# Gated attention and a feed-forward block on one core: pair 0 by token chunks, natural gates, one transfer queue and a new order

## The chip, the core and the metric

The kernel runs on one core of a Trainium2 chip. The metric is device time in microseconds of one execution, the median over runs. A profiled execution gives the span from the first to the last instruction and the busy time of each engine: PE (TensorE: matmuls and transposes; PEld is its weight load), DVE (VectorE), ACT (ScalarE), POOL (GpSimd), and SP (SyncE, which here only issues transfers). The transfers run on 16 DMA engines that all queues share.

## The reference

There are 4 batches, 8 heads, 768 tokens and 48 channels per head. A complex gate `a` with its magnitude capped at 0.999 decays a state per channel; `k` and `v` are added as an outer product, and `q` reads the state:

```python
mag = np.sqrt(a_re * a_re + a_im * a_im)
scale = np.minimum(mag, 0.999) / (mag + 1e-06)
for t in range(S):
    new_re = ar * S_re - ai * S_im
    new_im = ar * S_im + ai * S_re
    S_re, S_im = (new_re + einsum('bhd,bhe->bhde', k[t], v[t]), new_im)
    y[t] = einsum('bhd,bhde->bhe', q[t], S_re)
```

The heads' outputs are laid side by side (384 channels), and each token goes through a layer norm and a feed-forward block with a residual: `x + relu(norm(x) * g_ln @ w_ch1) @ w_ch2`, with 1536 hidden channels. Inputs and output are fp32.

## The kernel before

Tokens are handled in chunks of 128 (one token to a partition), and two chunks make a *pair*. A batch has three pairs, so there are 12 pairs, P = 0 to 11, and 24 chunks, n = 0 to 23. Pairs 0, 3, 6 and 9 begin a batch.

The recurrence is turned into matmuls. For a pair, the log magnitude `l` and the angle `th` of the gate are computed per token and channel; prefix sums over the tokens, which are matmuls with triangular ones, give the total decay and phase from the pair's start. Multiplying `k` and `q` by exponentials of these sums, and by cosine and sine, makes the recurrence an ordinary masked attention within the chunk plus a carried state `G`.

The steps of a pair have names that the plan uses, `name.P` or `name.n`, some with a part after them:

- `are`, `aim`, `q`, `k`, `vf`: loads. `ln`, `iv`, `r`: w = ln(re), 1/re, r = im/re. `r2`, `u`, `l`, `lc`: r squared, ln(1+r squared), half of it plus w, and the cap. `th`: arctan r.
- `dec`: matmuls that sum `l` over tokens; `e` and `en`: exponentials of plus and minus the sum. `ph`: the same sums of `th`, with the carry of the pair before; `sin`, `cos` (through `qt`, a quarter turn added on PE, or through `abs`); `car`: the carry to the next pair. `tab` loads ACT's function table (logarithms and exponentials, or trigonometry).
- `ke`, `qe`: k and q times the exponentials; `ks`, `qs`: times cosine and sine. `kT`, `qT` are transposes on PE and `ksT`, `qsT` their copies out of PSUM; where the plan gives `ksT` or `qsT` to SP, a transposing transfer does the whole step.
- `am`: scores, `atm`: scores times the mask, `gm`, `G`: the state, `y`: the output, `x`: its copy, `bn`: layer norm statistics, `rstd`: the inverse deviation, `xtr`, `xT`: x transposed.
- `mm1` (first product; three groups of four hidden blocks, two parts each), `relu`, `mm2` (second product, three parts for each chunk), `oa` and `ot`: scaling and residual, `st`: the store.
- `wl`, `wp`, `wc`: the weights are loaded as bf16 by POOL's queue, and g_ln and the mean's removal are folded into the first.

How the gates lie in SBUF matters for the change. `are` and `aim` are loaded so that a partition holds two *consecutive* tokens of the pair (a run of 384 B in DRAM). The sum for chunk c then takes both slots of every partition: `dec` is 2 x 2 matmuls with four triangular matrices `u_e[c, j]`, and `ph` likewise with `u_th`, plus one matmul for each chunk that adds the carry through `pick`. Pair 0 alone is cut in two parts by heads (`PARTS = {0: 2}`: four heads each), so that its first steps are shorter; both parts need both chunks of q and k.

The order is written by hand, as one list. A token `name:Ek` gives an operation to an engine (P = PE, A = ACT, V = DVE, G = POOL, S = SP) and, where it uses PSUM, to a bank; each engine runs its operations in the order of the list. A suffix `@other` makes an operation wait for another one ("turns at the shared port", for POOL and DVE). A transfer is issued by the engine that the token names, so that a wait in front of an issue holds up everything behind it in that queue. `warm.i` are fill-in matmuls that keep PE running and whose result isn't used. The buffers are rings (`RINGS`): three of `are`, `aim`, `q`, `k`, two of `vf`, five of `ot`.

Line 754 is `mm2`, 722 `mm1`, 617 `am`, 594 `kT` and `qT`, 688 `xtr`, 477 `dec`, 492 and 496 `ph`, 787 the fill-ins, 739 and 741 `relu`, 404 the loads of q, k and v, 445 those of the gates, 599 the transposing transfers, 777 the stores, 792 table loads, 770 `ot` on DVE; 295 and 292 are helpers for many of DVE's and POOL's products and copies.

Of the kernel before, what the change touches and what calls it, by code (L numbers as in the profile page):

```python
# [9 lines left out]
FP32 = mybir.dt.float32  # L10
# [24 lines left out]

ENGINES = {"P": "PE", "A": "ACT", "V": "DVE", "G": "POOL", "S": "SP"}
# [3 lines left out]
aim.0.0:A tab.log.0:A aim.0.1:A ue:G are.0.0:S are.0.1:S pad.e.1:G uth:V one:G warm.0:P0 pad.ks.0:G warm.1:P0  # L40
warm.2:P0 pick:G warm.3:P0 are.1.0:S warm.4:P0 warm.5:P0 warm.6:P0 k.0.1:S ln.0.0:A warm.7:P0 car0.1:G warm.8:P0
cmean:G iv.0.0:A warm.9:P0 ident:G warm.10:P0 warm.11:P0 r.0.0:V warm.12:P0 warm.13:P0 warm.14:P0 aim.1.0:S warm.15:P0
warm.16:P0 warm.17:P0 ln.0.1:A warm.18:P0 warm.19:P0 r2.0.0:A warm.20:P0 k.0.0:S warm.21:P0 warm.22:P0 warm.23:P0
warm.24:P0 u.0.0:A warm.25:P0 warm.26:P0 warm.27:P0 warm.28:P0 iv.0.1:A warm.29:P0 l.0.0:V warm.30:P0 are.2.0:S
warm.31:P0 warm.32:P0 ln.1.0:A warm.33:P0 warm.34:P0 r.0.1:G warm.35:P0 lc.0.0:V warm.36:P0 warm.37:P0 aim.2.0:S
warm.38:P0 warm.39:P0 warm.40:P0 iv.1.0:A warm.41:P0 warm.42:P0 pad.ks.1:G warm.43:P0 warm.44:P0 warm.45:P0 warm.46:P0
warm.47:P0 zdec:G r2.0.1:A warm.48:P0 pad.e.0:G warm.49:P0 pad.qs.0:G warm.50:P0 q.0.1:S warm.51:P0 warm.52:P0 u.0.1:A
warm.53:P0 warm.54:P0 r.1.0:V warm.55:P0 dec.0.0:P0 warm.56:P1 warm.57:P1 q.1.0:S e.0.0:A0 warm.58:P1 warm.59:P1
warm.60:P1 r2.1.0:V warm.61:P1 en.0.0:A0 warm.62:P1 warm.63:P1 warm.64:P1 l.0.1:V warm.65:P1 u.1.0:A warm.66:P1
warm.67:P1 warm.68:P1 warm.69:P1 lc.0.1:V warm.70:P1 are.3.0:S warm.71:P1 warm.72:P1 warm.73:P1 ln.2.0:A warm.74:P1  # L50
l.1.0:V warm.75:P1 warm.76:P1 warm.77:P1 warm.78:P1 dec.0.1:P6 q.1.1:S warm.79:P0 warm.80:P0 lc.1.0:V en.0.1:A6
warm.81:P0 warm.82:P0 warm.83:P0 warm.84:P0 q.0.0:S iv.2.0:A warm.85:P0 warm.86:P0 ke.0.1.0:G@lc.1.0 warm.87:P0
dec.1.0:P0 e.0.1:A6 r.2.0:V wl.1:G warm.88:P2 warm.89:P2 e.1.0:A0 warm.90:P2 warm.91:P2 warm.92:P2 warm.93:P2
warm.94:P2 gln:S r2.2.0:V en.1.0:A0 qrow:G dps.1:P4 dps.0:P5 ke.0.0.0:V warm.95:P2 warm.96:P2 u.2.0:A warm.97:P2
warm.98:P2 decc.1:V4 warm.99:P2 vf.0.0:S car0.0:G warm.100:P2 warm.101:P2 warm.102:P2 mask:G warm.103:P2 warm.104:P2
aim.3.0:S tab.trig.1:A warm.105:P2 warm.106:P2 warm.107:P2 wl.0:G qe.1.0.1:V warm.108:P2 warm.109:P2 vf.0.1:S
warm.110:P2 warm.111:P2 warm.112:P2 qe.1.0.0:V warm.113:P2 warm.114:P2 pad.qs.1:G warm.115:P2 warm.116:P2 l.2.0:V
th.0.0:A warm.117:P2 warm.118:P2 wl.2:G warm.119:P2 ph.0.0:P1 th.0.1:A th.1.0:A qe.0.0.0:V ph.0.1:P4 qe.0.1.0:V
warm.120:P0 warm.121:P0 warm.122:P0 k.1.0:S car.0.0:V1 decc.0:V5 sin.0.0:A1 lc.2.0:V sin.0.1:A4 qt.0.0:P1 ks.0.0.1:V
warm.123:P0 car.0.1:A4 wgc:V cos.0.0:A1 qt.0.1:P4 ph.1.0:P6 k.1.1:S ks.0.1.1:V cos.0.1:A4 qs.0.1.1:V th.2.0:A  # L60
# [153 lines left out]
def kernel(  # L214
# [14 lines left out]
    C = 128  # L229
# [73 lines left out]

    ident = pool.tile([C, C], BF16, name="ident")
    u_th = pool.tile([C, R, R, C], FP16, name="u_th")
    u_e = pool.tile([C, R, R, C], FP16, name="u_e")
    pick = pool.tile([C, C], FP16, name="pick")
    mask = pool.tile([C, C], BF16, name="mask")
    half_n = pool.tile([C, R], FP32, name="half_n")
# [514 lines left out]
```

## Time and profile before

| | |
|---|---|
| median of the runs | 191.07 us (190.74 to 191.28) |
| profiled execution | 192.75 us |
| its span | 191.0 us |
| PE, DVE, ACT, POOL busy | 177.3, 156.6, 158.9, 105.5 us |
| fill-in matmuls, busy | 17.5 us (134 of 256 columns) |
| transfers | 37.57 MB in 133080 packets |
| q1 (SP), q10 (ACT), q0 (POOL), share of 16 engines' span | 70.6%, 18.0%, 7.9% |

Busy time doesn't count issuing a transfer. Matmuls are pipelined: a row's mean duration is its latency, and the cost of one in a dense run is better read from the chain, where a piece such as four matmuls in 0.65 us gives their spacing. A DMA share sums packets that overlap, so that it can be over 1. A chain is followed back from the last instruction to whatever released each step.

### The profile page before, as it was taken

The numbers are of one execution on the slowest core, as the hardware profiler recorded it, in microseconds if no ns is written. First come the engines' busy times: TensorE is split into PE (matmuls) and PEld (weight loads), VectorE is DVE, ScalarE is ACT, GpSimd is POOL, SyncE is SP. The second block draws the span as 40 slices with busy tenths as digits, with TensorE's granted clock in tenths as the row PEclk, the third lists the DMA queues.
The fourth block names the chain that finished last, engine by engine and source line by source line (L and its number), as shares of the span: only waits on it lengthen the run. The fifth ranks groups of instructions, "written<-read, shape, count | busy, mean of one in ns | idle before, by whom it ended". The sixth has DMA issues, their size and how long they took to land.

```text
span 191.0 us, 5154 instructions
## 1 busy us (share of the span) xinstructions
PE 177.3 (93%) x2045; PEld 138.6 (73%) x2045; DVE 156.6 (82%) x285; ACT 158.9 (83%) x224; POOL 105.5 (55%) x124
## 2 busy tenths in 40 slices
PE   5999398999999999999968999999999999998992
PEld 3888365788667887776847687877867777786781
DVE  1678699999999999999996998998989867666532
ACT  3989499999999997899949999998999979662340
POOL 7419032579196899071539483347785954940130
PEclk9999999999999999999999999999999999999998
DMA  6999999999969999889999999999799979994032
GB/s 153 278 240 202 212 198 204 210 214 207 242 108 287 205 220 234 154 183 234 136 265 234 190 221 230 282 223 204 141 160 262 217 126 179 256 191 151 5 124 82
DMA packets 133080, 37.57 MB, mean 197 GB/s; under 512 B 127168, under 2 KB 133056, under 8 KB 133056
## 3 DMA queue, kind: packets, MB, share of 16 engines
q1 hardware_dynamic: 107760, 27.21, 70.6%
q10 hardware_dynamic: 22512, 7.67, 18.0%
q0 software_dynamic: 2784, 2.36, 7.9%
q8 instruction: 16, 0.26, 0.6%
q14 instruction: 8, 0.07, 0.1%
HBM read 28.31 MB, written 4.72 MB: 173 GB/s over the span
## 4 chain that ended last, share of the span: by engine, by line
PE 63%; DVE 10%; ACT 9%; DMA 8%; issue 4%; ACTq 2%; POOL 1%; SPq 1%; DVEq 0%; POOLq 0%
PE banks L754 22%; PE banks L722 16%; PE banks L617 5%; PE banks L594 4%; DMA q<-in_q_dram 4%; DMA ksT<-ks 3%; PE banks L477 3%; PE banks L667 2%; ACTq L777 2%; PE banks L496 2%; PE banks L670 2%; DVE w1b L388 2%; DMA are<-in_a_re_dram 2%; PE banks L645 2%; PE banks L688 2%
## 5 line engine op out<-in xcount | busy, mean ns | idle before, releaser
L754 PE MATMUL banks<-w2b,h 128*128 128x384 bf16 (+1 forms) x300 | 55.7, 319 | 0.6 <-ACT h L739 0.6
L722 PE MATMUL banks<-xT,w1b 128*128 128x256 bf16 x432 | 50.9, 272 | 0.7 <-ACT h L739 0.5
L722 PEld LDWEIGHTS <-w1b 128*128 128x128 bf16 x432 | 41.4, 98 | 7.0 <-issue 1.2
L754 PEld LDWEIGHTS <-h 128*128 128x128 bf16 x300 | 26.7, 97 | 13.8 <-ACT h L739 1.0
L295 DVE TENSOR_TENSOR atm<-banks,mask 128x1024 bf16<-128x1024 f32 x24 | 29.0, 1219 | 3.8 <-PE banks L617 2.9
L739 ACT ACTIVATE h<-banks 128x1024 bf16<-128x1024 f32 (+1 forms) x26 | 25.7, 1009 | 4.6 <-DVE ks L295 2.6
L792 ACT ACT_TABLE_LOAD x19 | 24.4, 1283 | 2.6 <-PEq L808 1.3
L295 POOL TENSOR_TENSOR ke<-k,en 128x384 bf16<-128x384 f32 x17 | 15.4, 916 | 14.1 <-ACT e L481 4.3
L767 POOL TENSOR_TENSOR ot<-ot,x 128x384 f32<-128x384 f32 x13 | 12.5, 967 | 14.2 <-ACT ot L760 12.9
L295 POOL TENSOR_TENSOR r<-aim,are 128x768 f16<-128x768 f32 (+1 forms) x8 | 13.7, 1715 | 11.0 <-DVE w1b L388 4.1
L787 PE MATMUL banks<-u_e 128*128 128x256 f16 x134 | 17.5, 286 | 2.2 <-POOL u_e L323 2.2
L295 POOL TENSOR_TENSOR qs<-qe,trig 128x768 bf16<-128x768 bf16 x8 | 13.0, 1640 | 10.3 <-DVE w1b L388 7.2
L617 PE MATMUL banks<-qsT,ksT 128*128 128x128 bf16 x192 | 14.5, 219 | 2.8 <-ACT h L739 2.1
L787 PEld LDWEIGHTS <-u_e 128*128 128x128 f16 x134 | 13.5, 102 | 4.5 <-POOL u_e L323 1.9
L617 PEld LDWEIGHTS <-ksT 128*128 128x128 bf16 x192 | 12.1, 97 | 5.1 <-issue 2.8
L741 DVE TENSOR_SCALAR h<-banks 128x1024 bf16<-128x1024 f32 (+1 forms) x11 | 12.7, 1166 | 2.7 <-PE banks L722 2.7
L295 POOL TENSOR_TENSOR qe<-q,e 128x384 bf16<-128x384 f32 x12 | 11.0, 917 | 6.8 <-DVE r L295 3.6
L466 DVE SCALAR_TENSOR_TENSOR l<-r,w 128x768 f16<-128x768 f16 (+1 forms) x13 | 12.6, 969 | 1.3 <-ACT r L462 1.1
L680 DVE BATCH_NORM_STATS2 stats<-x 128x6 f32<-128x384 bf16 x24 | 13.1, 546 | 0.1
L667 PE MATMUL banks<-v,atm 128*128 128x48 bf16 x192 | 12.0, 183 | 0.0
L514 ACT ACTIVATE trig<-banks 128x768 bf16<-128x768 int16 (+1 forms) x13 | 9.8, 761 | 2.5 <-DVE car L509 2.4
L496 PE MATMUL banks<-th,u_th 128*128 128x384 f16 (+1 forms) x52 | 11.8, 313 | 0.0
(93 smaller groups left out, 380.8 us busy)
## 6 DMA issues: line engine op xcount, KB each, us to landing
k<-in_k_dram SPq DMA_DIRECT2D x24, 192.0 KB, 5.1
q<-in_q_dram SPq DMA_DIRECT2D x24, 192.0 KB, 4.3
are<-in_a_re_dram SPq DMA_DIRECT2D x11, 384.0 KB, 5.1
aim<-in_a_im_dram SPq DMA_DIRECT2D x11, 384.0 KB, 5.0
out_dram<-ot ACTq DMA_DIRECT2D x19, 192.0 KB, 3.4
vf<-in_v_dram ACTq DMA_DIRECT2D x18, 192.0 KB, 4.3
w1b<-in_moe_w_ch_dram POOLq DMA_DIRECT2D x3, 384.0 KB, 7.6
vf<-in_v_dram SPq DMA_DIRECT2D x6, 192.0 KB, 7.0
```

Of the source, the lines that this page charges most:

```text
L295: {"DVE": nc.vector, "POOL": nc.gpsimd}[eng(name)].tensor_tensor(**kw)
L466: nc.vector.scalar_tensor_tensor(out=S_("l"), in0=S_("r2"), scalar=0.5, in1=S_("w"), op0=ALU.mult, op1=ALU.add)
L496: nc.tensor.matmul(heads(ps[:, c]), lhsT=u_th[:, c, j], rhs=step(T("th", P), j), start=False, stop=(j == R - 1), skip_group_check=True)
L617: nc.tensor.matmul(ps[:, h], lhsT=T("ksT", n)[:, h], rhs=T("qsT", n)[:, h], start=True, stop=True)
L667: nc.tensor.matmul(ps[:, h], lhsT=T("atm", n)[:, h], rhs=T("v", P)[:, c, h], start=True, stop=nfirst)
L680: nc.vector.bn_stats(out=T("stats", n), in_=T("x", n))
L722: nc.tensor.matmul(ps[:, jj], lhsT=w1b[:, dc, ts(gi * JG + jj, C)], rhs=T("xT", P)[:, dc].rearrange("p c t -> p (c t)"), start=(dc == 0), ...
L739: act(out=dst, in_=src, func=AF.Relu)
L741: nc.vector.tensor_scalar(out=dst, in0=src, scalar1=0.0, scalar2=None, op0=ALU.max)
L754: nc.tensor.matmul(bank(own)[:, 0:w], lhsT=T("h", P)[:, j, ts(c, C)], rhs=w2b[:, j, es], start=(j == 0), stop=(j == NJ - 1))
L787: g.add(f"warm.{i}", lambda i=i: nc.tensor.matmul(bank(f"warm.{i}")[:, 0:256], lhsT=u_e[:, 0, 0], rhs=u_e[:, 1].rearrange("p j t -> p (j t ...
L792: g.add(f"tab.{nm}.{i}", lambda tab=tab: nc.scalar.preload_act_table_set(tab))
```

## The change

- **Pair 0 by token chunks.** Its two parts are now its two chunks of 128 tokens with all eight heads, no longer its two halves of the heads. Each chunk has its own loads of `are` and `aim`; chunk 0 needs only the first chunk of q and k. The second chunk's sums take `l` and `th` of both.
- **Direct log magnitude for pair 0.** `sa`, `sb`, `sc` compute re squared, im squared and their sum in fp32, in the space of pair 1's `h` buffer; `u` is its logarithm, `lc` halves and caps it. `r2` and `l` are gone for pair 0, and the `relu`s of pair 1 wait for `u` of pair 0.
- **Natural gates.** For pairs 0 and 4 to 11 a partition holds token p of chunk 0 and token p of chunk 1, so the loads are per chunk with runs of 192 B (one token). Two new matrices, `n_e` and `n_th` (triangular, and all ones), replace the four: chunk 0 sums one slot and chunk 1 two, three matmuls in place of four.
- **Transfers on SP.** All loads of `vf` and all stores are issued by SP; ACT keeps the first two loads, `are.0.0` and `aim.0.0`. `xT.18` and `xT.22` become transposing transfers, and one more `ksT` does.
- **A new order** for all engines, with other engines for some operations and two more table loads.
- **Fill-ins**: 61 of 512 columns in place of 134 of 256.

The diff, cut (the plan is all new; some of its lines are kept here):

```diff
+DIRECT = {0}
+CHUNKED = {0}
+NATURAL = {0, 4, 5, 6, 7, 8, 9, 10, 11}
...
-aim.0.0:A tab.log.0:A aim.0.1:A ue:G are.0.0:S are.0.1:S pad.e.1:G uth:V one:G warm.0:P0 pad.ks.0:G warm.1:P0
...
+ue:G pad.qs.0:G are.0.1:S uth:V are.0.0:A aim.0.0:A pick:G gln:S tab.log.0:A ln.0.0:A ln.0.1:A sa.0.0:V iv.0.0:A
+sb.0.0:G sa.0.1:A sc.0.0:V ident:G car0.0:G@sa.0.0 u.0.0:A aim.0.1:S sb.0.1:V are.1.0:S q.0.1:S ln.1.0:A sc.0.1:V
+u.0.1:A aim.1.0:S iv.1.0:A ne:G lc.0.0:V r.0.0:V k.0.1:S car0.1:G warm.0:P0 warm.1:P0 warm.2:P0 warm.3:P0 warm.4:P0
...
+r.1.0:V aim.2.0:S mask:G pad.qs.1:G k.0.0:S r2.1.0:V iv.0.1:A r.0.1:V pad.ks.1:G@r2.1.0 e.0.1:A0 vf.0.0:S u.1.0:A
+tab.trig.1:A th.0.1:A wl.0:G qe.0.1.0:V th.0.0:A q.0.0:S qrow:G@qe.0.1.0 l.1.0:V lc.1.0:V th.1.0:A warm.20:P1
...
+am.14:P2 atm.14:V2 e.9.0:A6 ln.11.0:A gm.14:P0 q.9.1:S iv.11.0:A vf.8.1:S st.7:S st.8:S q.9.0:S mm2.12.1:P5 rstd.6:A
...
+    def c_ne():
+        nc.gpsimd.memset(n_e, 1.0)
+        nc.gpsimd.affine_select(out=n_e[:, 0], in_=n_e[:, 0], pattern=[[1, C]],
+                                compare_op=ALU.is_ge, fill=0.0, base=0, channel_multiplier=-1)
...
+            cc = [i] if cw else list(range(R))
...
+            def step(t, j, hs=hs, nat=nat):
+                if nat:
+                    return t.rearrange("p h x -> p (h x)")[:, ds(j * DM, DM)].rearrange(
+                        "p (h d) -> p h d", d=D)
                 return t[:, hs].rearrange("p h (j d) -> p h j d", j=R)[:, :, j]
+
+            def sums(c, step_t, nat_t, nat=nat):
+                if nat:
+                    return [(nat_t[:, 0 if j == c else 1], j) for j in range(c + 1)]
+                return [(step_t[:, c, j], j) for j in range(R)]
...
+                elif nat:
+                    for c in range(R):
+                        add(f"{nm}.{X}.{c}", lambda nm=nm, ap=ap, X=X, c=c, step=step: ring(
+                            f"{nm}.{X}.{c}").dma_start(out=step(T(nm, P), c), in_=ap[b].rearrange(
+                                "h (c p) d -> p c h d", p=C)[:, pp * R + c]), uses=[(nm, P)])
...
+                add(f"u.{X}", lambda S_=S_, sq=sq: act(out=S_("r2"), in_=sq[:, 0], func=AF.Ln,
+                                                       scale=1.0 + 2.0 * LNEPS),
+                    needs=[f"sc.{X}"], uses=[("r2", P)])
...
-                for c in range(R):
-                    for j in range(R):
-                        nc.tensor.matmul(heads(ps[:, c]), lhsT=u_e[:, c, j], rhs=step(T("l", P), j),
-                                         start=(j == 0), stop=(j == R - 1))
+                for c in cc:
+                    parts = sums(c, u_e, n_e)
+                    for i, (lhsT, j) in enumerate(parts):
+                        nc.tensor.matmul(heads(ps[:, c - cc[0]]), lhsT=lhsT, rhs=step(T("l", P), j),
+                                         start=(i == 0), stop=(i == len(parts) - 1))
...
-    for i in range(134):
+    for i in range(61):
         g.add(f"warm.{i}", lambda i=i: nc.tensor.matmul(
-            bank(f"warm.{i}")[:, 0:256], lhsT=u_e[:, 0, 0], rhs=u_e[:, 1].rearrange(
-                "p j t -> p (j t)"), start=True, stop=True), needs=["ue"], ps=(f"warm.{i}", 1))
+            bank(f"warm.{i}"), lhsT=u_e[:, 0, 0], rhs=u_e.rearrange("p c j t -> p (c j t)"),
+            start=True, stop=True), needs=["ue"], ps=(f"warm.{i}", 1))
```

More of the change, by code (lines that the diff above doesn't have):

```diff
@@ L43 @@
[L43 to L52, printed above, removed]
@@ L742, in f_relu @@
                                                 op0=ALU.max)
-                add(name, f_relu, needs=[f"mm1.{P}.{gi}.{x}" for x in ((s,) if end else (0, 1))],
+                add(name, f_relu, needs=[f"mm1.{P}.{gi}.{x}" for x in ((s,) if end else (0, 1))]
+                    + ([f"u.0.{i}" for i in range(PARTS[0])] if P == 1 else []),
                     uses=[("h", P)], ps=(o, 2))
```

363 lines of the change are left out of this document (207 added, 156 removed).

## The prediction

> **What bounds the kernel now.** I read the page's busy shares first, then stages of the span, then the chain of waits in order of time, then idle gaps and DMA queues. The page:
>
> ```profile
> span 191.0 us, 5154 instructions
> PE 177.3 (93%) x2045; PEld 138.6 (73%) x2045; DVE 156.6 (82%) x285; ACT 158.9 (83%) x224; POOL 105.5 (55%) x124
> ```
>
> The stages (PE, PEld, DVE, ACT and POOL busy us, then granted clock, DMA share, GB/s):
>
> ```profile
> 0.00:10.00 10.00, 7.78 (x59) 6.40 (x60) 4.37 (x5) 6.82 (x11) 5.91 (x24) 1.00 0.87 220
> 10.00:20.00 10.00, 9.86 (x106) 8.59 (x104) 7.37 (x14) 9.25 (x14) 5.53 (x10) 1.00 1.06 214
> 20.00:30.00 10.00, 6.44 (x63) 4.28 (x62) 8.89 (x24) 7.53 (x12) 1.64 (x1) 1.00 1.12 209
> 30.00:40.00 10.00, 9.46 (x136) 7.55 (x134) 9.98 (x17) 9.79 (x14) 5.60 (x5) 1.00 0.94 201
> 40.00:50.00 10.00, 10.00 (x133) 8.57 (x131) 9.57 (x17) 9.73 (x14) 7.13 (x9) 1.00 1.20 228
> 49.70:187.00 137.30, 133.84 (x1564) 103.39 (x1561) 115.72 (x211) 116.12 (x163) 79.67 (x76) 1.00 0.97 193
> 180.00:191.00 11.00, 7.21 (x67) 5.88 (x64) 3.50 (x7) 2.88 (x7) 2.70 (x3) 0.92 0.26 91
> 0.00:165.00 165.00, 155.71 (x1795) 121.70 (x1796) 143.45 (x262) 149.59 (x207) 98.68 (x118) 1.00 1.05 209
> ```
>
> There are three stages. Up to about 30 us PE mostly runs fill-ins while pair 0 is prepared. From 30 to 50 us DVE and ACT are full. From 49.70 to 187.00 PE is busy 133.84 of 137.30 us, so there it is the bound, with 3.46 us of idle. DMA has packets in flight nearly all the way to 165 us: a share of 1.05 (packets overlap, so the scale passes 1). The chain, in order of time (start, us, what):
>
> ```profile
> 13.77 7.08 DMA q<-in_q_dram
> 49.74 2.03 PE banks L754 x12
> 52.39 0.65 PE banks L754 x4
> 53.04 0.65 PE banks L477 x4
> 56.47 0.45 PE banks L594 x8
> 59.67 0.33 PE banks L496 x2
> 71.10 0.73 ACTq L777
> 131.75 0.34 PE banks L688 x6
> 171.20 1.60 ACTq L777
> ```
>
> It waits 7.08 us for q of pair 0, reaches the second matrix product (L754, mm2.0.0) at 49.74, and is mostly PE from there, with two pieces of store issues on ACT's queue (71.10 and 171.20). I use 49.74 as the milestone: time up to it, PE's work behind it, what PE loses, the tail.
>
> **The change, part by part.**
>
> *Natural gates, on PE.* For pairs 4 to 11 the prefix sum of l goes from 4 matmuls to 3, that of th from 4 to 3 (the carry's two stay). Four L477 take 0.65 us, two L496 0.33: 0.163 each. 16 matmuls fewer: 2.6 us of PE, nearly all behind the milestone, where PE is the bound. Three transposes leave PE for DMA (kT one fewer, 0.45; xtr two fewer, 0.34 for two): 0.8. The new order puts one more transpose (qT.4, 0.45) ahead of mm2.0.0. PE's work behind the milestone: -2.6 -0.8 -0.5 = -3.9 us. Pair 0's own gates (twenty matmuls of 192 columns before, eight of 384 after) lie among the fill-ins ahead of the milestone: 0.
>
> *Natural gates, on DMA.* The runs of are and aim are 384 B (two tokens) now and become 192 B in nine pairs: 18 tiles of 384 KB, 1024 more packets each, 16 more issues. Two stretches price it: 98 to 100 us has aim's 384 B tiles alone, 88 to 90 us rows of 192 B alone, apart from a few packets:
>
> ```profile
> DMA packets 1678, 0.64 MB, mean 319 GB/s; under 512 B 1678, under 2 KB 1678, under 8 KB 1678
> DMA packets 2436, 0.47 MB, mean 236 GB/s; under 512 B 2428, under 2 KB 2436, under 8 KB 2436
> 88.00:90.00 2.00, 2.00 (x34) 1.41 (x32) 2.00 (x4) 1.99 (x3) 0.00 (x0) 1.00 1.16 236
> 98.00:100.00 2.00, 0.68 (x5) 0.29 (x3) 1.87 (x4) 0.26 (x1) 0.43 (x1) 1.00 1.17 319
> ```
>
> A tile of 393 KB takes 393/319 = 1.23 us as it is, 393/236 = 1.67 as 192 B rows: +0.43, times 18 = 7.8 us. The three added transposes (ksT's 256 KB, two of x's 96 KB) are 0.46 MB, about 1.5 us at 319. So 9.3 us of full-rate transfer are added. Before moves a share of 1.05 for 165 us where full rate shows 1.16: 173 of 191 possible. After needs about 184 (9.3 x 1.16 = 10.8 more) in some 161 us, a share of 1.14. That fits under 1.16 with nothing to spare. From below it costs 0 (prefetch hides it all, as DMA waits in before are small). From above, if 1.05 is all that the kernel's own order of issues and waits lets through, 184/1.05 = 175, so +10. I take +1.5, near the lower end, because the 40 to 50 us stage held 1.20 for 10 us.
>
> The Trainium skill, DMA: Bandwidth & Descriptors (Why small descriptors are slow), gives a fixed 3 cycles for each packet beside 1 for each 32 B: 2 x (6+3) = 18 against 12+3 = 15, so 1.2 times as long. The trace's rows give 319/236 = 1.35, and the measurement decides; by the page the term would be 4.4 us instead of 7.8 and the sum would be about 0.6 us lower.
>
> *Transfers on SP.* 18 loads of v and 19 stores leave ACT's queue. Their issue rows, with SP's:
>
> ```profile
> L404 ACTq DMA_DIRECT2D vf<-in_v_dram x18: 374/401/641, 56.0 to 162.1; - x18
> L777 ACTq DMA_DIRECT2D out_dram<-ot x19: 338/363/2372, 70.4 to 173.6; - x19
> L404 SPq DMA_DIRECT2D k<-in_k_dram x24: 533/1158/3460, 2.4 to 148.4; - x24
> L445 SPq DMA_DIRECT2D are<-in_a_re_dram x13: 454/747/2487, 0.8 to 118.6; - x13
> L599 SPq DMA_TRANSPOSE ksT<-ks x14: 1232/1354/2945, 54.1 to 163.0; - x14
> SPq L599 <- DVE ks L295: 14.3, 4, 6.6
> 75.87 1.47 PE L722 MATMUL banks<-xT,w1b 128*128 128x256 bf16 x12 [0.47 <-ACT h L739]
> 174.73 0.82 PE L754 MATMUL banks<-w2b,h 128*128 128x384 bf16 x4 [0.59 <-ACT h L739]
> ```
>
> ACT's queue loses 18 x 0.40 + 19 x 0.36 = 14 us. Most of that shortens nothing, since PE is the bound. Where it did show, ACT stood behind a store (71.10, 171.20) and PE then idled 0.47 and 0.59 us for a relu: I book -1.1. SP goes from 110 issues to 166: 34 loads at 0.45 to 1.16 us (ends of the are and k rows), 19 stores at about 0.36, three transposes at 1.35: 26 to 50 us more on one queue that works in order. It is hidden while SP runs ahead of the consumers. The new waits are for stores: st.8 waits for ot.8, and behind it stand q.9.0, two transposes and vf.8.0, on which qe and then qs of pair 9 wait. A wait of this kind is in before already (SP stood up to 6.6 us at one transpose). Its price is part of the +1.5 above.
>
> *Pair 0 by token chunks, direct log magnitude.* In place of r2 (ACT) and l (DVE), each chunk gets two squares and a sum off the raw inputs:
>
> ```profile
> L295 DVE TENSOR_TENSOR r<-aim,are 128x384 f16<-128x384 f32 x1 | 0.6, 559 | 2.2 <-ACT are L450 2.2
> L295 POOL TENSOR_TENSOR r<-aim,are 128x384 f16<-128x384 f32 x1 | 1.0, 1000 | 2.8 <-ACT are L450 2.8
> L466 DVE SCALAR_TENSOR_TENSOR l<-r,w 128x384 f16<-128x384 f16 x2 | 1.1, 554 | 1.1 <-ACT r L462 1.1
> L462 ACT ACTIVATE r<-r 128x384 f16<-128x384 f16 x2 | 1.0, 522 | 0.1
> L787 PE MATMUL banks<-u_e 128*128 128x256 f16 x134 | 17.5, 286 | 2.2 <-POOL u_e L323 2.2
> L792 ACT ACT_TABLE_LOAD x19 | 24.4, 1283 | 2.6 <-PEq L808 1.3 <-issue 0.9
> ```
>
> DVE pays 4 x 0.56 for squares and sums and saves 2 x 0.55; POOL pays one square (1.0), ACT swaps two r2 for one square (-0.5), with two table loads more (+2.6, spread over the span). But the log no longer waits for ln, iv, r, r2 in turn. The larger effect is q of the first chunk: the transfers up to it hold 3072 KB instead of 3840 (pairs 2 and 3 wait), and at 214 GB/s the missing 786 KB are 3.7 us. So y.0 comes several us sooner. Does the milestone? Adding the rows of every DVE and ACT instruction that the two orders put ahead of mm2.0.0, I get as estimates for DVE 38.9 us before and 38.2 after, for ACT 43.3 and 45.1. ACT idled 6.9 us in the first 50 (10 minus each row) and can regain part of the 3.7. I book -0.5, with +3 (ACT's extra and another late load) and -3 (the wait for q gone altogether) as ends.
>
> *Rest of the order.* Some 40 instructions change engine (abs 4 and G 2 from ACT to DVE, v from DVE to POOL and ACT, two ks and two qe to POOL). By the same rows DVE nets about +1.4 us, POOL +2.5, ACT about 0 beside its issues. All three have room behind the milestone (115.72, 116.12 and 79.67 of 137.30): 0. If DVE's cover went, its whole 1.4 would be paid. The 61 fill-ins of 512 columns take 4/3 of the 0.163 of a 384 column one, 0.22 each, 13 us against 17.5 busy: nothing waits on them, 0.
>
> *Tail.* Now three last sums run behind the last matmul:
>
> ```profile
> 186.66 1.27 DVE L770 SCALAR_TENSOR_TENSOR ot<-banks,rstd,x 128x384 f32<-128x384 f32 x3 [2.17 <-PE banks L754]
> ```
>
> After, only one half (about 0.4 of the 1.27) does: -0.4, between -0.9 and 0.
>
> Sum: -0.5 -3.9 +1.5 -1.1 -0.4 = -4.4. The profiled execution took 192.75 us (span 191.0), which becomes 188.35; the median of the runs is 191.07, 1.7 lower, and with the same difference becomes 186.67, so 186.7.
>
> **The rivals.** *DMA becomes the bound (slower).* One queue in order, stalled behind stores and transposes, with 10.8 more to move: if it sustains 1.10, between 1.05 and 1.16, the loads end at 184/1.10 = 167 against 165, and the end moves with them, since what follows the last load changes little: about +2.5, 193.6. It decides below a share of 184/165 = 1.115. For it: 1.05 was the mean even with two queues. Against: SP's queue alone gave 319 GB/s at 98 us.
>
> *The early start counts in full.* The milestone 3 us sooner, and PE's remaining idle halved: -3 -3.9 -1.7 -0.4 = -9, with DMA hidden: about 182. For it: the 7.08 us wait. Against: DVE and ACT full from 30 to 50.
>
> *The start gives nothing, as ACT and DVE set the milestone.* +3 on the sum's -0.5: 190.2, hardly faster.
>
> *The clock falls in the start.* Fewer fill-ins leave PE idle longer. In 20 to 30 us PE was busy 6.44 at clock 1.00, but 180 to 191, with idle at its end, shows 0.92. If one 10 us stage fell to half, its few real matmuls (about 3 us) would double: +3, 189.7. The Trainium skill, TensorE: Matmul & The Clock Gate (What's actually happening), has the clock halved after an idle window of about 3.4 us; the new order spreads its first 36 fill-ins in two blocks, and no run here yet shows the gaps between.
>
> **How the numbers follow.** Forecast 0.45 (184.5 to 189); DMA as the bound 0.26; early start in full 0.15; start gives nothing 0.08; clock 0.06. The predicted time is the first's. The range reaches from the early start (182.5) to just past the DMA rival (194.5). A measurement can tell about 0.3%, 0.6 us. Faster 0.68, same 0.05, slower 0.27: the last is the DMA rival and a little of the two before it.
>
> **What would show it.** Right: mm2.0.0 at 48 to 50 us; 16 fewer L477 and L496; DMA share near 1.14 with PE idle under 4 us behind the milestone; no store issues on ACT's queue. Wrong: PE idle released by DMA or by transposes over 6 us, loads still running past 166 us, mm2.0.0 past 52, a clock under 1.00 before 40 us.

## The result and the profile after

The changed kernel takes 204.27 us (median; 203.91 to 206.01), against 191.18 us for the kernel before: a ratio of 1.070, 95% interval 1.063 to 1.077. It is 13 us slower. The prediction said 186.7 us, in a range of 182.5 to 194.5, and gave "slower" 0.27: wrong in sign and outside its range. Ratios, here and below, take the fast executions alone, so a ratio can differ from the quotient of two medians. The profiled execution of before lay 1.6 us above its median (192.75) and that of after 0.4 (204.63), so the spans differ by 11.7 us and not by 13.

The page of the kernel after: span and busy time of each engine, DMA totals, the queue of SP, the chain's shares.

```profile
span 202.7 us, 4968 instructions
PE 177.8 (88%) x1925; PEld 129.1 (64%) x1928; DVE 161.6 (80%) x284; ACT 158.8 (78%) x224; POOL 111.0 (55%) x127
DMA packets 153655, 38.01 MB, mean 187 GB/s; under 512 B 147744, under 2 KB 153632, under 8 KB 153632
q1 hardware_dynamic: 148768, 34.94, 88.3%
PE 41%; DMA 19%; ACT 15%; SPq 12%; DVE 8%; issue 3%; DVEq 0%; ACTq 0%
```

DMA totals, the queue of SP and the chain's shares of the kernel before:

```profile
DMA packets 133080, 37.57 MB, mean 197 GB/s; under 512 B 127168, under 2 KB 133056, under 8 KB 133056
q1 hardware_dynamic: 107760, 27.21, 70.6%
PE 63%; DVE 10%; ACT 9%; DMA 8%; issue 4%; ACTq 2%; POOL 1%; SPq 1%; DVEq 0%; POOLq 0%
```

PE's busy time is about what it was (177.8 us against 177.3) in a span that is 11.7 us longer. In the chain that ended last, PE has fallen from 63% to 41%, and DMA has risen from 8% to 19%; SP's own issuing, 1% before, is 12%. The bytes hardly differ (38.01 MB against 37.57), the packets do: 153655 against 133080.

The stages of the kernel after (window, length, then busy us of PE, PEld, DVE, ACT, POOL, granted clock, DMA share, GB/s). The sixth runs from the first to the last start of the second matrix product, as 49.70 to 187.00 did before:

```profile
0.00:10.00 10.00, 7.78 (x25) 3.14 (x26) 4.16 (x9) 5.71 (x10) 6.67 (x21) 1.00 0.98 199
10.00:20.00 10.00, 7.58 (x44) 3.68 (x42) 7.91 (x14) 9.10 (x16) 5.81 (x11) 1.00 1.19 236
20.00:30.00 10.00, 7.91 (x110) 4.99 (x110) 8.80 (x14) 8.82 (x13) 6.54 (x10) 1.00 1.04 189
30.00:40.00 10.00, 7.66 (x76) 4.96 (x74) 8.33 (x17) 6.53 (x10) 6.72 (x11) 1.00 1.20 204
40.00:50.00 10.00, 8.17 (x96) 6.15 (x97) 6.38 (x10) 8.07 (x10) 5.07 (x4) 0.83 1.05 185
56.60:199.50 142.90, 132.02 (x1526) 100.90 (x1524) 119.41 (x209) 114.06 (x162) 74.69 (x68) 1.00 0.96 185
0.00:165.00 165.00, 144.35 (x1553) 103.16 (x1557) 136.95 (x240) 141.53 (x198) 100.25 (x114) 0.99 1.05 198
```

The milestone of the prediction, the start of mm2.0.0, and the last issues of v stand in two answers on single lines of the kernel after (columns: shortest, median and longest duration in ns, first and last start in us):

```profile
L839 PE MATMUL banks<-w2b,h x300: 246/326/337, 56.6 to 199.5; 128*128 128x384 bf16 x138, 128*128 128x192 bf16 x12
```

```profile
L425 SPq DMA_DIRECT2D vf<-in_v_dram x24: 377/698/1892, 7.6 to 177.1; - x24
```

From these rows and those of before the 11.7 us of span split into four, which the prediction had as terms:

| part of the span | before | after | change | predicted |
|---|---|---|---|---|
| up to the milestone | 49.7 | 56.6 | +6.9 | -0.5 |
| PE busy behind it | 133.84 | 132.02 | -1.8 | -3.9 |
| PE idle behind it | 3.46 | 10.88 | +7.4 | +0.4 (DMA +1.5, ACT's queue -1.1) |
| from the last matmul's start to the end | 4.0 | 3.2 | -0.8 | -0.4 |

The two parts that PE and the tail own went the right way. Two others cost 14 us. The last load of v, which was issued at 162.1 before, is issued at 177.1, and the DMA engines moved 198 GB/s up to 165 us where they moved 209: their share is the same 1.05, with less moved in it.

The chain of the kernel after, in order of time, shows DMA pieces from end to end (start, us, what):

```profile
13.48 7.68 DMA are<-in_a_re_dram
31.84 8.65 DMA vf<-in_v_dram
40.51 0.84 ACT v L433
96.76 3.47 DMA vf<-in_v_dram
118.02 4.08 DMA ksT<-ks
129.06 3.63 DMA vf<-in_v_dram
142.32 5.81 DMA aim<-in_a_im_dram
171.55 5.52 DMA ksT<-ks
```

The wait for q of pair 0 (7.08 us before) is gone, and in its place are.2.0 lands at 21.16: its log stands ahead of other work in ACT's queue. Next vf.1.1, issued at 31.84, lands at 40.49. The list of waits names what engines stood for (engine, line, releaser: us in total, times, longest), first POOL's two longest waits for loads, then PE's three longest behind the milestone:

```profile
POOL ke L299 <- DMA k<-in_k_dram: 11.4, 4, 6.4
POOL ke L299 <- DMA vf<-in_v_dram: 5.8, 1, 5.8
```

```profile
PE banks L701 <- DMA ksT<-ks: 2.6, 2, 1.4
PE banks L701 <- DVE r L299: 2.5, 1, 2.5
PE banks L701 <- DMA qsT<-qs: 1.0, 2, 0.6
```

Before, POOL waited for a load only once, and PE's longest wait behind the milestone was for ACT:

```profile
POOL v L414 <- DMA vf<-in_v_dram: 1.4, 1, 1.4
PE banks L617 <- ACT h L739: 2.1, 1, 2.1
```

Of PE's 10.88 us of idle the profile puts 3.6 on DMA transposes directly. The rest is behind ACT and DVE; POOL, which computes ke ahead of them, stood 11.4 + 5.8 = 17.2 us for loads itself. That PE's other idle comes from POOL's waits is likely, but the list doesn't show it.

### The profile page after: what moved, and what is told of

The parts are those of the page before. It is cut to its first block, busy times and chain, and to the rows that moved or that the text cites. A ratio compares the mean times of both kernels' runs of the same rounds, so it can differ in the third digit from the quotient of the medians.

```text
span 202.7 us, 4968 instructions
## 1 busy us (share of the span) xinstructions
PE 177.8 (88%) x1925; PEld 129.1 (64%) x1928; DVE 161.6 (80%) x284; ACT 158.8 (78%) x224; POOL 111.0 (55%) x127
## 2 busy tenths in 40 slices
DMA packets 153655, 38.01 MB, mean 187 GB/s; under 512 B 147744, under 2 KB 153632, under 8 KB 153632
## 3 DMA queue, kind: packets, MB, share of 16 engines
q1 hardware_dynamic: 148768, 34.94, 88.3%
## 4 chain that ended last, share of the span: by engine, by line
PE 41%; DMA 19%; ACT 15%; SPq 12%; DVE 8%; issue 3%; DVEq 0%; ACTq 0%
PE banks L839 16%; PE banks L806 9%; DMA vf<-in_v_dram 8%; SPq L425 5%; DMA ksT<-ks 5%; PE banks L701 4%; DMA are<-in_a_re_dram 4%; ACT h L823 3%; SPq L492 3%; DMA aim<-in_a_im_dram 3%; PE banks L678 2%; PE banks L751 2%; DVE atm L299 2%; ACT trig L598 1%; PE banks L577 1%
## 5 line engine op out<-in xcount | busy, mean ns | idle before, releaser
L839 PE MATMUL banks<-w2b,h 128*128 128x384 bf16 (+1 forms) x300 | 54.3, 319 | 0.3 <-ACT h L823 0.3
L299 DVE TENSOR_TENSOR atm<-banks,mask 128x1024 bf16<-128x1024 f32 x24 | 28.9, 1220 | 9.0 <-PE banks L701 8.1
L299 POOL TENSOR_TENSOR ke<-k,en 128x384 bf16<-128x384 f32 x17 | 15.8, 935 | 26.1 <-DMA k<-in_k_dram 11.4
L872 PE MATMUL banks<-u_e 128*128 128x512 f16 x61 | 17.8, 428 | 3.8 <-POOL u_e L329 2.2
L701 PEld LDWEIGHTS <-ksT 128*128 128x128 bf16 x192 | 12.5, 100 | 9.8 <-issue 5.2
L299 POOL TENSOR_TENSOR r<-aim,are 128x768 f16<-128x768 f32 x7 | 13.1, 1871 | 7.5 <-DMA aim<-in_a_im_dram 3.2
L299 POOL TENSOR_TENSOR qs<-qe,trig 128x768 bf16<-128x768 bf16 (+1 forms) x8 | 12.4, 1552 | 7.3 <-DVE qe L299 3.0
L852 POOL TENSOR_TENSOR ot<-ot,x 128x384 f32<-128x384 f32 x12 | 11.1, 938 | 8.6 <-ACT ot L845 7.5
L299 POOL TENSOR_TENSOR qe<-q,e 128x384 bf16<-128x384 f32 x14 | 13.6, 975 | 3.7 <-ACT e L561 1.1
L299 POOL TENSOR_TENSOR ks<-ke,trig 128x768 bf16<-128x768 bf16 (+1 forms) x7 | 11.8, 1687 | 4.6 <-PE banks L839 2.9
L872 PEld LDWEIGHTS <-u_e 128*128 128x128 f16 x61 | 6.3, 107 | 11.8 <-issue 6.7
L825 DVE TENSOR_SCALAR h<-banks 128x1024 bf16<-128x1024 f32 (+1 forms) x10 | 11.4, 1160 | 2.2 <-PE banks L806 2.2
L299 DVE TENSOR_TENSOR ks<-ke,trig 128x768 bf16<-128x768 bf16 (+1 forms) x19 | 12.1, 653 | 0.9 <-POOL ke L299 0.8
L751 PE MATMUL banks<-v,atm 128*128 128x48 bf16 x192 | 11.7, 183 | 1.2 <-DVE ot L855 0.7
L299 POOL TENSOR_TENSOR r<-r 128x768 f16<-128x768 f16 x5 | 7.4, 1476 | 9.3 <-DVE r L299 9.2
```

What stands on the lines that cost most here:

```text
L299: {"DVE": nc.vector, "POOL": nc.gpsimd}[eng(name)].tensor_tensor(**kw)
L701: nc.tensor.matmul(ps[:, h], lhsT=T("ksT", n)[:, h], rhs=T("qsT", n)[:, h], start=True, stop=True)
L751: nc.tensor.matmul(ps[:, h], lhsT=T("atm", n)[:, h], rhs=T("v", P)[:, c, h], start=True, stop=nfirst)
L825: nc.vector.tensor_scalar(out=dst, in0=src, scalar1=0.0, scalar2=None, op0=ALU.max)
L839: nc.tensor.matmul(bank(own)[:, 0:w], lhsT=T("h", P)[:, j, ts(c, C)], rhs=w2b[:, j, es], start=(j == 0), stop=(j == NJ - 1))
L852: nc.gpsimd.tensor_tensor(out=T("ot", n)[:, es], in0=T("ot", n)[:, es], in1=T("x", n)[:, es], op=ALU.add)
```

## The experiments

Three theories could explain this. N: runs of 192 B instead of 384 B for pairs 4 to 11 cost the DMA engines more time than there was. Q: one queue in order (SP) holds loads behind stores and transposes. O: the order of the first issues makes the start late. A fourth, I, came up on the way: the sheer number of issues on SP. Each ratio is against the kernel before on the same chip, with its 95% interval.

**Loads of v and stores given back to ACT.** 37 of SP's 166 issues: loads of v from pair 3 on, and the same 19 stores as before, on ACT's queue again:

```diff
-vf.3.1:S
+vf.3.1:A
...
-st.19:S
+st.19:A
```

> The changed kernel, with the loads of vf of pairs 3 to 11 and 19 of the stores issued by ACT again, at the places that the new order gives them; nothing else differs. Theory Q (one queue: SP's 166 issues in order are what holds the loads back): most of the 13 us of loss goes, 193 to 197 us. Theory N (short runs: the 192 B rows of pairs 4 to 11 fill the DMA engines, whoever issues them): 202 to 206 us. Theory O (the order of the first transfers: SP issues what pairs 2, 3 and 4 need ahead of vf.1.1): 202 to 206 us, since the first 50 us are hardly touched.

Measured: 206.48 us, 1.079 (1.071 to 1.088). Nothing comes back. Q as the main cause falls for this order: the wait behind stores, which the prediction had feared, isn't where the time went.

**Long runs.** The changed kernel with pairs 4 to 11 loaded as before, each are and aim in one transfer where the second of the two stood:

```diff
-NATURAL = {0, 4, 5, 6, 7, 8, 9, 10, 11}
+NATURAL = {0}
...
-are.4.0.1:S
...
-are.4.0.0:S
+are.4.0:S
...
```

> The changed kernel, with pairs 4 to 11 back to runs of 384 B and the four gate matrices (natural gates for pair 0 alone); each pair's two loads become one at the place of the second. Theory N: 194 to 198 us. Theory Q: 16 issues fewer of 166, 201 to 204 us. Theory O: 202 to 205 us, as only the loads of pair 4 fall in the first 50 us. If PE were the bound, the 16 matmuls that come back would add 2.6 us.

Measured: 193.93 us, 1.016 (1.009 to 1.023). 10.3 of the 13 us come back (1.070 - 1.016 = 0.054 of 191). The run also goes back to four matmuls for each sum and drops the 16 added issues; experiments below tell these apart. Its page, its stretch from the first to the last start of the second matrix product with its first 165 us, and its loads of v, in three fences:

```profile
DMA packets 137015, 38.01 MB, mean 197 GB/s; under 512 B 131104, under 2 KB 136992, under 8 KB 136992
q1 hardware_dynamic: 132128, 34.94, 89.2%
```

```profile
53.80:189.60 135.80, 132.97 (x1541) 102.64 (x1540) 116.25 (x209) 113.92 (x162) 74.08 (x68) 1.00 0.97 194
0.00:165.00 165.00, 154.66 (x1663) 111.94 (x1667) 143.29 (x258) 149.41 (x209) 104.71 (x121) 0.99 1.06 209
```

```profile
L423 SPq DMA_DIRECT2D vf<-in_v_dram x24: 368/738/2029, 8.4 to 167.0; - x24
```

PE's idle behind the milestone is 135.80 - 132.97 = 2.8 us, less than before the change (3.46), and the last v is issued 10 us earlier than in the changed kernel. What stays is the start: 53.8 against 49.7.

**The short runs alone, in the old order.** The kernel before with the natural gates of pairs 4 to 11 (loads split in place, three matmuls for each sum), and nothing else:

```diff
-are.4.0:S
+are.4.0.0:S are.4.0.1:S
...
 pad.qs.2:G
+ne:G nth:V
...
-aim.11.0:S
+aim.11.0.0:S aim.11.0.1:S
```

> The kernel before, with natural gates for pairs 4 to 11 alone (16 loads more, 16384 packets more, 16 matmuls fewer, the two constants made on POOL and DVE at 48 us). Theory N: 197 to 203 us. Theory Q and theory O: 188.5 to 192 us, the 2.6 us of PE gained or hidden.

Measured: 196.57 us, 1.032 (1.024 to 1.039). N again, just under the 197 to 203 that it said. In the old order the part costs 6 us, not 10. The stretch of the second matrix product, the first 165 us, and the queue of SP:

```profile
48.60:189.00 140.40, 131.26 (x1542) 101.60 (x1540) 118.52 (x212) 115.99 (x163) 79.09 (x76) 1.00 1.03 193
0.00:165.00 165.00, 151.70 (x1747) 119.00 (x1750) 142.89 (x259) 146.02 (x200) 95.86 (x117) 1.00 1.10 204
```

```profile
q1 hardware_dynamic: 124400, 27.21, 76.1%
```

The milestone, 48.6, is not late here: what the short runs cost in this order is PE's idle behind it, 140.40 - 131.26 = 9.1 us against 3.46. And DMA's share up to 165 us is 1.10, above the 1.05 of the changed kernel.

**The move to SP alone.** The kernel before with all loads of v and all stores on SP:

```diff
-vf.3.0:A
+vf.3.0:S
...
-st.19:A
+st.19:S
```

> The kernel before, with all loads of vf and all stores on SP at their places in the order; nothing else differs. Theory Q: 196 to 203 us. Theory N and theory O: 190 to 192 us.

Measured: 189.78 us, 0.997 (0.993 to 1.000). Alone the move does no harm, and is perhaps worth half a microsecond. The Trainium skill, DMA: Bandwidth & Descriptors (Issuing engines are not separate DMA queues), says that transfers issued by several engines run on the same 16 DMA engines, and that more issuers save only the time to issue. This run (0.997, with 37 issues more on SP) and the first (1.079 against 1.070, with 37 fewer) agree with it.

**The first issues reordered.** The changed kernel with are.2.0, k.1.0, q.1.0 and vf.1.1 issued sooner:

```diff
+are.2.0:S
 aim.2.0:S
...
-are.2.0:S
...
+k.1.0:S q.1.0:S vf.1.1:S
 are.3.0:S
...
-k.1.0:S
...
-q.1.0:S
...
-vf.1.1:S
```

> The changed kernel with three things moved on SP near the start: are.2.0 is issued ahead of aim.2.0, and k.1.0, q.1.0 and vf.1.1 are issued ahead of are.3.0. Theory O (the order in which the first transfers are issued loses the start): vf.1.1 lands by about 36 us instead of 40.5 and mm2.0.0 starts by about 52 us instead of 56.6, total 198 to 201. Theory N (the short runs load the DMA engines, and the order only says who waits): something else is late in its place, total 203 to 205, within 0.5% of the changed kernel.

Measured: 204.67 us, 1.067 (1.059 to 1.075). The same stretch as above:

```profile
54.20:199.20 145.00, 133.91 (x1525) 101.91 (x1524) 119.77 (x209) 114.21 (x162) 74.80 (x68) 0.99 0.95 185
```

The milestone comes at 54.2, 2.4 us sooner, and the end at 202.4, 0.3 sooner: PE is idle 145.00 - 133.91 = 11.1 us behind the milestone. The lead was given back while PE waited. A start that is 2.4 us sooner doesn't make the end sooner here; O, as far as these moves test it, falls as a cause of the total.

**The same reorder with long runs.**

```diff
-NATURAL = {0, 4, 5, 6, 7, 8, 9, 10, 11}
+NATURAL = {0}
...
+are.2.0:S
 aim.2.0:S
...
+k.1.0:S q.1.0:S vf.1.1:S
 are.3.0:S
...
```

> The changed kernel with runs of 384 B and four triangle matmuls for pairs 4 to 11 (as in e2_long_runs, 193.9) and the same three moves on SP as in e5_start. Theory O: it gains another 2 to 4 us, 189.5 to 192. Theory N alone: the start is not held by the order, 193 to 194.5.

Measured: 196.50 us, 1.024 (1.015 to 1.033). Nor do these moves help where the loads keep up: the time is above what either theory expected and not under the 1.016 of the long runs alone, and mm2.0.0 starts at 54.4, no sooner than their 53.8.

**The matmuls alone.** The kernel before with three matmuls for each gate sum of pairs 4 to 11, on the old layout:

```diff
+ne:G nth:V
...
+            def sums(c, step_t, nat_t, nat=P >= 4):
+                if nat:
+                    return [(nat_t[:, 0 if j == c else 1], j) for j in range(c + 1)]
+                return [(step_t[:, c, j], j) for j in range(R)]
...
```

> The kernel before with three triangle matmuls instead of four for each gate sum of pairs 4 to 11, on the old layout with runs of 384 B: the matmul half of the natural gates without their short transfers. The gates of pairs 4 to 11 are then summed over the wrong tokens, so this part of the computation is changed. If TensorE bounds that stretch, the 16 matmuls less are worth up to 2.6 us: about 188.5. If the work is hidden behind something else: 190.5 to 191.2.

Measured: 191.17 us beside 192.34 of the kernel before, 0.998 (0.992 to 1.003): -0.5 us, between -1.5 and +0.5. The 16 matmuls less are worth 2.6 us by their rows; the full value lies outside the interval. The two new constants are made in this run too, so they aren't what makes the natural gates slow.

**The transfers alone.** The kernel before with short runs but four matmuls (the two constants are made, and not used):

```diff
-are.4.0:S
+are.4.0.0:S are.4.0.1:S
...
+            def sums(c, step_t, nat_t, nat=False):
...
```

> The kernel before with the loads of pairs 4 to 11 in runs of 192 B (two transfers for each of their are and aim), and four triangle matmuls as before: the transfer half of the natural gates without their saving on TensorE. The rows land in other places, so the gates of pairs 4 to 11 are summed over the wrong tokens. Theory N: no faster than e3_before_natural (196.6), and up to 2.6 us slower if the saving on TensorE counted there: 196.5 to 199.5. If the natural gates cost e3_before_natural its time in another way (the order of its matmuls, the new constants), this one stays near the kernel before: 190.5 to 192.

Measured: 198.88 us beside 192.34, 1.026 (1.016 to 1.037): +5 us. Three stretches of this kernel:

```profile
60.00:80.00 20.00, 17.41 (x237) 14.73 (x235) 18.26 (x31) 16.56 (x23) 15.60 (x15) 0.97 1.09 215
100.00:120.00 20.00, 17.87 (x220) 13.78 (x218) 17.47 (x32) 17.08 (x25) 13.54 (x13) 1.00 1.26 217
120.00:140.00 20.00, 17.86 (x225) 13.76 (x223) 15.87 (x31) 15.90 (x23) 7.78 (x10) 1.00 1.21 203
```

and the same three before:

```profile
60.00:80.00 20.00, 19.53 (x261) 16.53 (x260) 19.55 (x35) 18.25 (x26) 15.95 (x15) 1.00 0.96 213
100.00:120.00 20.00, 19.18 (x250) 14.85 (x250) 17.09 (x32) 19.22 (x28) 12.49 (x12) 1.00 1.16 219
120.00:140.00 20.00, 20.00 (x238) 16.18 (x237) 18.29 (x36) 19.05 (x26) 12.77 (x13) 1.00 1.06 202
```

DMA's share rises by 0.10 to 0.15 and the GB/s hardly do: packets are in flight longer for the same bytes, and PE is 2.1, 1.3 and 2.1 us less busy there. The short transfers by themselves account for the loss of the natural gates in this order (1.026 beside 1.032).

**Packets or issues?** The changed kernel with long runs, but each load still in two transfers, split by heads:

```diff
-NATURAL = {0, 4, 5, 6, 7, 8, 9, 10, 11}
+NATURAL = {0}
...
+elif P >= 4:
+    for c in range(2):
+        add(f"{nm}.{X}.{c}", lambda nm=nm, ap=ap, X=X, c=c: ring(
+            f"{nm}.{X}.{c}").dma_start(out=T(nm, P)[:, ts(c, H // 2)], in_=ap[b][
+                ts(c, H // 2)].rearrange("h (k p j) d -> p k h (j d)", p=C, j=R)[:, pp]),
+            uses=[(nm, P)])
...
```

> The changed kernel with pairs 4 to 11 in runs of 384 B and four triangle matmuls (as in e2_long_runs, 193.9), but with each of their are and aim loads still split into two transfers, by heads, at the two places where the changed kernel issues them: as many issues on SP as the changed kernel (166), but half as many packets for these loads. Theory N (number of packets): like e2_long_runs, 192.5 to 195.5. Theory I (the number of issues on SP: 175 us of SP's time are issues in the changed kernel, 157 us in e2_long_runs): like the changed kernel, 201 to 205.

Measured: 196.45 us, 1.022 (1.014 to 1.031), a little above the expected 192.5 to 195.5, and 9 us below the changed kernel.

```profile
DMA packets 137271, 38.01 MB, mean 193 GB/s; under 512 B 131360, under 2 KB 137248, under 8 KB 137248
```

With as many issues as the changed kernel and the packets of the long runs, the time goes with the packets. I falls as the main cause; it may own one or two microseconds. The time that SP spends on issues doesn't explain the loss either: summed over each trace it is 175.0 us in the changed kernel, 165.1 here and 157.3 with long runs, but 152.0 in the first experiment, which was as slow as the changed kernel.

**Both parts in the old order.** The short runs of the third experiment with the queues of the fourth:

```diff
-vf.3.0:A
+vf.3.0:S
...
-st.19:A
+st.19:S
```

> The kernel before with natural gates for pairs 4 to 11 (e3_before_natural, 196.6) and with all vf loads and stores on SP as well (e4_before_sp, 189.8). If the two add: 194.5 to 197. If the single queue makes the short runs dearer, which neither run alone could show, and this is why they cost 10 us in the changed kernel but 6 us in the old order: 199 or more.

Measured: 202.01 us, 1.048 (1.041 to 1.055). The two don't add: 1.032 times 0.997 would be 1.029. The stretch where its profile is behind first:

```profile
20.00:40.00 20.00, 14.72 (x152) 10.13 (x152) 16.00 (x35) 14.70 (x22) 4.32 (x3) 0.83 1.00 190
```

and the same in the kernel before with the move to SP alone:

```profile
20.00:40.00 20.00, 18.02 (x216) 13.92 (x217) 19.81 (x42) 19.58 (x29) 8.96 (x9) 1.00 1.10 217
```

This is not yet an interaction shown: PE is 3.3 us behind, at a granted clock of 0.83, in a stretch in which both kernels issue nearly the same transfers (the first short tile, are.4.0, is issued at 28.7), at 190 GB/s against 217. So the two halves of the move were tried one by one, again on the kernel before with natural gates for pairs 4 to 11. Loads of v alone on SP:

```diff
-vf.3.0:A
+vf.3.0:S
...
-vf.11.0:A
+vf.11.0:S
```

> The kernel before with natural gates for pairs 4 to 11 (e3_before_natural, ratio 1.032) and with the vf loads alone on SP as well; the stores stay on ACT. If moving vf ahead of and between the short loads is what e11_sp_natural (ratio 1.048) pays: ratio 1.043 to 1.052, 200 to 202. If not: 1.028 to 1.036, 197 to 199.

Measured: 197.41 us, 1.030 (1.021 to 1.040). Stores alone on SP:

```diff
-st.0:A
+st.0:S
...
-st.19:A
+st.19:S
```

> The kernel before with natural gates for pairs 4 to 11 (e3_before_natural, ratio 1.032) and with the stores alone on SP as well; vf stays on ACT. If the stores, which wait for their tile in SP's order, hold the short loads behind them: ratio 1.043 to 1.052, 200 to 202. If not: 1.028 to 1.036, 197 to 199. If neither this nor e15_vf_sp is above 1.036, only both together make it, or the two do not add for another reason.

Measured: 195.25 us, 1.019 (1.009 to 1.029). Neither is dearer than the short runs with two queues (1.032). Why both together took 202 stays open, and with it whether one queue makes the short runs dearer.

**Half the dose.** The changed kernel with short runs for pairs 8 to 11 alone:

```diff
-NATURAL = {0, 4, 5, 6, 7, 8, 9, 10, 11}
+NATURAL = {0, 8, 9, 10, 11}
```

> The changed kernel with short runs left for pairs 8 to 11 alone; pairs 4 to 7 back to runs of 384 B and four matmuls. If each short tile costs the same (about 10 us over eight pairs): 198 to 200. If the loss is made at the start, where pairs 4 to 7 are loaded beside the last inputs of pairs 1 to 3: 193.5 to 196.5. If it is made late: 201 to 204.

Measured: 198.80 us, 1.033 (1.026 to 1.040). Between 1.016 with none and 1.070 with eight pairs, the last four pairs cost 0.017 and the first four 0.037. The loss isn't made in one place: it grows with the number of short tiles. Whether the first four cost more because they are early, or because they come on top of the others, this run can't tell.

**The log magnitude alone.** The kernel before with all loads of v and stores on SP (0.997) and pair 0's logarithm from re^2+im^2:

```diff
+DIRECT = {0}
...
+sa.0.0:V
...
+sb.0.0:V sc.0.0:V u.0.0:A
...
+lc.0.0:V
...
-r2.0.0:A
...
-u.0.0:A
...
-l.0.0:V
...
-lc.0.0:V
...
```

> The kernel before with all vf loads and stores on SP (e4_before_sp, 189.8) and with the log magnitude of pair 0 from re^2+im^2 at once, in the two halves by heads that pair 0 has there; nothing else of the change. Three squares and sums take the place of two instructions for each half, off the reciprocal's chain. If the chain through the reciprocal sets pair 0's start and with it the end: 188 to 189.3. If the start is held by transfers and VectorE's queue: 189.5 to 191.5.

Measured: 193.14 us, 1.007 (1.002 to 1.011), a loss of about 1% against the same kernel without it, and slower than either expectation. The chain through the reciprocal isn't what holds the start in the old order. VectorE, whose queue gets three instructions for one in each half, is the likely place; that was not tried by itself.

**DMA time taken away elsewhere.** The changed kernel, all short runs kept, with its 26 DMA transposes of ks and qs replaced by plain copies of the same bytes (the expectation miscounts them as 24):

```diff
-nc.sync.dma_start(out=T(src + "T", n),
+nc.sync.dma_start(out=T(src + "T", n).rearrange("p h x -> p (h x)"),
-                  in_=T(src, P)[:, c].rearrange("p h x -> p (h x)"),
-                  transpose=True)
+                  in_=T(src, P)[:, c].rearrange("p h x -> p (h x)"))
```

> The changed kernel with its 24 DMA transposes of ks and qs replaced by plain copies of the same bytes at the same places on SP, 2 KB for each partition: the same issues and waits, but far fewer packets. The attention of those chunks is then computed from tiles that are not transposed. If the time of the DMA engines is what the short runs use up: 190 to 198, though all short runs are still there. If each short load is late by itself, whatever else the engines do: 201 to 204.

Measured: 192.14 us, 1.008 (1.004 to 1.013). Its page, the stretch of the second matrix product with the first 165 us, and its loads of v:

```profile
DMA packets 129943, 38.01 MB, mean 199 GB/s; under 512 B 120704, under 2 KB 126592, under 8 KB 129920
q1 hardware_dynamic: 125056, 34.94, 79.2%
```

```profile
53.40:187.60 134.20, 131.20 (x1525) 100.77 (x1524) 117.68 (x209) 113.77 (x162) 74.12 (x68) 1.00 0.83 201
0.00:165.00 165.00, 153.92 (x1658) 110.56 (x1659) 146.08 (x259) 150.08 (x209) 106.14 (x122) 0.99 0.98 213
```

```profile
L425 SPq DMA_DIRECT2D vf<-in_v_dram x24: 405/789/2183, 7.6 to 163.8; - x24
```

The bytes, the short loads, the order and the queue are those of the changed kernel; 23712 packets are gone from another place. The last v is issued at 163.8 instead of 177.1, PE idles 134.20 - 131.20 = 3.0 us behind the milestone instead of 10.88, and 12 us come back. So the short loads are not late by themselves: with other packets taken away they no longer make the end late. What the two have in common is the time of the DMA engines; on SP's queue the packets took 179.0 us before this edit (88.3% of 202.7) and 151.1 with it (79.2% of 190.8).

Two other things change in this run. A plain copy lands a little sooner than a transpose (medians 3.5 and 3.1 us against 3.9 and 4.0), and it is issued faster: SP's issues sum to 149.0 us instead of 175.0. Against the second as the reason stand the first experiment, with 152.0 us of issues and no gain, and the split long runs, with 165.1 and a gain of 9 us. Plain copies with long runs weren't run. There PE idles only 2.8 us behind the milestone, so a gain of 12 us from the copies alone isn't likely, but that is an argument and not a run.

No version beat the kernel before by more than the measurement can tell; nearest is the move to SP alone, 0.997 (0.993 to 1.000).

## Why the prediction was wrong

*Natural gates, on DMA: this step failed; its term was mis-sized.* It took +1.5 us out of 0 to +10, near the lower end, "because the 40 to 50 us stage held 1.20 for 10 us". The runs show 10.3 us for the 16 short tiles of pairs 4 to 11 in the new order (1.070 with them, 1.016 without) and 6 us in the old one (1.032). The loads aren't hidden: PE's idle behind the milestone is 10.88 us with short runs and 2.8 without in the new order, 9.1 against 3.46 in the old. And the share that the step needed, 1.14, never lasted to 165 us: it is 1.05 in the changed kernel, 1.10 and 1.08 in the two runs with short runs in the old order and two queues. A peak of ten microseconds was taken for what the kernel can hold.

That the upper end, +10, came so close is in part luck. It was the time for 18 tiles and three transposes if 1.05 is all that the order lets through. But 1.05 is no fixed limit: up to 165 us the old order held 1.10 with the same 16 tiles, and 1.00 with all transfers on SP as well (time ratio 1.048); the new order held 1.08 with 37 issues back on ACT, and was no faster (1.079). Packet time isn't a fixed price of a tile either. On SP's queue the 16 tiles added 6.9 us in the new order (179.0 against 89.2% of 192.9, 172.1), where the step's own figures give 16 x 0.43 x 1.16 = 8.0; in the old order they added 12.5 (76.1% of 193.6 against 70.6% of 191.0) and cost less. Why the same tiles cost 10 us in the new order and 6 in the old stays open. The step also priced the transposes as plain bytes. By the run with plain copies, a transpose of 256 KB takes (179.0 - 151.1)/26 = 1.07 us of packet time more than a copy of the same bytes; for three added ones that is a small term.

The end goes with the last load: from the last issue of v to the end it is 28.9 us before (191.0 - 162.1), 25.6 after, 25.9 with long runs and 27.0 with plain copies, while the last issue itself moves by 15 us. This alone doesn't tell which of the two follows the other; the run with plain copies speaks for the loads.

For the size of a short tile the prediction had 1.35 times as long by rates, and weighed one rule of the Trainium skill against it, the fixed cycles of each packet, which gives 1.2. It left out another of the same page (DMA: Bandwidth & Descriptors, How a descriptor splits into AXI transactions): a run that doesn't start at a multiple of 256 B is fetched from the boundary below. By that, taking the tensors to begin at such a boundary, runs of 192 B fetch 192, 384, 320 and 256 B in turn (9 beats of 32 B on average) and runs of 384 B fetch 384 or 512 (14); with three cycles for each packet, an estimate of 2 x 12 = 24 against 17, 1.41. The trace's 1.35 lies between the two. No run here changed the alignment alone.

*The rival "DMA becomes the bound"* had the mechanism, and named its sign: this is the case that came. Its size was wrong for the same reason: it set the sustained share at 1.10, halfway between 1.05 and 1.16, and came out at 193.6. With 1.05 it would have been 184/1.05 = 175 for the last load, the +10 above: about 201 by its own sum. The half of it that blamed one queue in order is not borne out by the first and fourth experiment; beside short runs in the old order (1.048) it stays open.

*Start: wrong as well.* -0.5 was booked, with +3 as the upper end; the milestone came 6.9 us later. Of that 2.8 us go with the short runs (56.6 against 53.8 with long runs), in this order alone: with short runs in the old order the milestone is at 48.6. The other 4.1 belong to the new order and pair 0's chunks, near the rival "the start gives nothing, as ACT and DVE set the milestone" (+3). Where in the new order they arise was not separated: giving vf.1.1 and are.2.0 earlier issues did not lower the total. The direct logarithm, tried alone in the old order, cost 1% rather than gaining.

*Natural gates, on PE.* -3.9 was booked; PE's busy time behind the milestone fell by 1.8, and the 16 matmuls alone were worth 0.5 us (at most 1.5). The step took PE as the bound because it was busy 133.84 of 137.30 us. In the profile of the run with the matmuls alone the same stretch is 135.1 us with 131.6 busy, both 2.2 less, so there the saving shows; that the time fell by so much less isn't explained by any run.

*ACT's queue* was booked at -1.1. The move alone gave 0.997, which is -0.6 us (-1.3 to 0), and PE's idle behind the milestone is 0.6 lower with long runs than before: at most about half of what was booked shows, and no gain is clear of noise. *Tail*: -0.4 booked, -0.8 came. *Fill-ins and the clock*: the granted clock was 0.83 in 40 to 50 us, at 8.17 us of busy PE at most 1.4 us (8.17 x 0.17); the rival that priced it at +3 was a contributor at best. Two executions of the changed kernel took the same 203.91 us at mean granted clocks of 0.974 and 0.992.

*What would show it wrong*: loads past 166 us (issued to 177.1) and the milestone past 52 (56.6) came. PE's idle grew to 10.88 us, though only 3.6 of it is released by transposes directly, so its sign has to be read through the engines between. The clock fell after 40 us, not before.

## What to carry to other kernels

Where transfers are in flight for most of the span, ask whether the kernel has ever held the share that the added packets need for the whole of that time. A stage's peak doesn't answer it: 1.20 for ten microseconds stood beside a mean of 1.05, and with short runs and the transposes kept the mean came to 1.00 to 1.10, depending on order and queues. Where the end of the range was worked out from the kernel's own mean, the booked value should lie well inside the range, not next to the other end. A DMA row that stays busy while its GB/s fall says that the same bytes now take more packet time. Halving a run's length to save matmuls spends a resource that transposes and stores share; test it by taking packets away somewhere else.

## What was not expected of the hardware

- Twenty-six DMA transposes of 256 KB (bf16, 128 x 1024) against plain copies of the same bytes: 23712 packets more and, with the short runs there, 12 us of the kernel's time.
- DMA's share can stay the same while the rate falls: 1.05 at 209 GB/s before, 1.05 at 198 after. The share counts time with packets in flight, not bytes moved.
- Which engine issues a transfer made no difference that shows in two of three comparisons (0.997 with 37 issues more on SP in the old order; 1.079 against 1.070 with 37 fewer in the new), though SP's issues sum to 175.0 of 202.7 us.
- The third is the exception: the short runs with all transfers on SP took 202.0 us in the old order (1.048 against 1.032 with two queues), and neither half of the move explains it (197.4 and 195.3). This is left open.
